# Orders of TensorE, VectorE and ScalarE written out by places of one product, and MLP2 weights converted in place, in a fused attention and two-MLP kernel

## The chip, the cores and the metric

The kernel runs on one core of a Trainium2 chip. The metric is the device time of one launch in microseconds (us); the launches of the kernel before took 960.7, 959.1 and 956.2 us, median 959.1.

The engines of a core run side by side, each through its own queue in order: TensorE (PE in the profile) multiplies matrices into PSUM, VectorE (DVE) and ScalarE (ACT) work on tiles in SBUF and PSUM, GpSimd (POOL) does a few small steps, and SyncE (SP) issues the DMAs. An instruction that waits holds up all that stand behind it in the queue of its engine.

## What is computed

```python
# q, k, v: (4 batches, 8 heads, 768 positions, 64); 8 memory keys per head
for c in range(S // 32):                       # attention in chunks of 32 queries
    k_full = [mem_k, k[l_start:r_end]]         # 8 memory keys, 16 left, 32 own, 8 right
    v_full = [mem_v, v[l_start:r_end]]
    a = softmax(q_c @ k_full.T / sqrt(64))
    out[c] = a @ v_full
x = out as (3072 tokens, 512)
x = ((x @ w_a) * (x @ w_b)) @ w_out            # MLP1: 512 -> 1536 -> 512
h = x @ w_in                                   # MLP2: 512 -> 1024
solu = h * softmax(h)
ln = (solu - mean) / sqrt(var + 1e-6) * g_ln
return ln @ w_out2                             # 1024 -> 512
```

All is float32. The weights of the MLPs reach the chip as the eight-byte words of float64 numbers and are converted there. A product in float32 is made of three matmuls: each operand is cut into a high part (a rounded copy, made on ACT) and a low part (what is left, made by a subtraction on DVE), and high x low, low x high and high x high are summed in PSUM.

## The kernel before

**Tiling.** The 3072 tokens are six blocks of 512. Attention goes by 24 groups of 128 queries, four to a block; a group has the steps load, `P`, `S` (64 small matmuls), `M` (maximum, exponent), `X` (transposes of the block's result before it), `N` (sums, and a multiplication of tile `EB` on GpSimd), `T`, `V` and `L`. Blocks 0 and 1 go straight through MLP1 in twelve steps `f`, each with 128 of the 1536 hidden columns: `ab` makes x @ w_a and x @ w_b, `gate` multiplies them, ACT casts the high part `gh`, `gate_lo` makes the low part, and `x2_step` multiplies by w_out and adds up.

**Strassen steps.** Blocks 2 to 5 go as two superblocks of two blocks, by a scheme of seven products (Strassen, in Winograd's form) in place of eight, again by twelve hidden tiles: together 24 steps, g = 0 to 23. A step g has seven `s_product`s of six 128x512 matmuls each (this takes one **place** below), in the order s_1, s_2, s_6, s_7, s_5, s_3, s_4. Between them the accumulators are snapped: ACT copies after s_1, s_6 and s_5 (lines 501, 510, 519) into three rotating buffers (`part`: G0, u2, u4, so each copy needs the buffer that an earlier step's split has finished reading), and DVE adds (506, 520, 524, 530) and multiplies (the rest of 524 to 531). The two results of a step are cut into high (ACT, 495) and low (DVE, 496) parts. From g = 2 on each step also holds four **thirds** of six matmuls, that multiply the results of step pairs before it by w_out and add to `acc` (ACT copy 550, DVE add 552).

**Operands.** For the scheme the weights of each f are first combined by sums on DVE (`s1_sums`, lines 379 and 390) and cut (`s1_split`, 396 and 397) during the second block, and travel through DRAM (`wsa`, `wsb`). The x operands need sums too (`t1_sums`, 434) and splits (`x1_op`, 444 and 445): once ahead of the first superblock, from tick 64 of the second block on, and once more between the superblocks, in step g = 11 (`last`).

**MLP2's weights.** From g = 12 on, `w2_jobs_of` gives four jobs to each step. A conversion loads 128 rows (512 KB) of raw words, takes `w_abs` (ACT, 283), `w_low` (ACT, 286), `w_range` (DVE, 296 and 297), `w_sign` (304) and `w_add` (312); w_out2's pieces are multiplied by g_ln (DVE, 623); w_in2's are also combined for the seven products by `w2_sub`. `w2_store` casts (ACT, 578), subtracts (DVE, 579) and stores the piece to DRAM (`w2s`, 22 pieces); when the places in SBUF are free, `w2_place` loads each back. w_in2 comes first, w_out2 last.

**MLP2.** Twelve pairs j of token tiles: `h_load`, `h_sums` (GpSimd), `h_split` (721, 722), then seven `product`s (`h_p1`, `h_a1`, `h_a2`, `h_b1`, `h_b2`) with running maxima (DVE, 759), `soft_exp`, `soft_stats`, `soft_scale` per tile (817 to 855), `h_norm`, the transposes `t_mm` (865), a split of them (870, 871) and `o_mm`, 24 matmuls by w_out2. At the transition, the last eight thirds run among the first products of pair 0.

**What sets the order.** TensorE's order is that of the program text throughout. VectorE's and ScalarE's is so only up to line 1059; behind it, a scheduler orders these two by its own estimate of times, with a few `issue_after` lines for the jobs. Attention steps are hung on a counter that `tick()` moves on once per place.

Of the kernel before, what the change touches and what calls it, by code (L numbers as in the profile page):

```python
# [18 lines left out]
P = 128  # L19
# [35 lines left out]
def fused_kernel(  # L55
# [23 lines left out]
    w2s = [dram.tile([P, 2, WC], F32, name=f"w2s{i}") for i in range(14 + NF2)]  # L79
# [295 lines left out]
    def s1_sums(q):  # L375
# [6 lines left out]
        )  # L382
        z = s1[q].rearrange("p (i c) -> p i c", i=4)
# [8 lines left out]
    def s1_split(q):  # L392

        l = s1.pop(q)
        h = Z[:, 4 * WC:6 * WC]
        nc.scalar.copy(h.bitcast(F32R), l)
        nc.vector.tensor_tensor(out=l.bitcast(F32R), in0=l, in1=h, op=ALU.subtract)
        for k, t in enumerate((h, l)):
            t = t.rearrange("p (i c) -> p i c", i=4)
            nc.sync.dma_start(wsa[q][:, 2:4, k], t[:, 0:4:3])  # L400
            nc.sync.dma_start(wsb[q][:, 0:2, k], t[:, 1:3])
# [24 lines left out]
    def t1_sums():  # L426

        a, b = stage(0), stage(1)
        t1, t2, t4 = (
            ld_tile(2 * TB, "t").rearrange("d (k t) -> d k t", k=2) for _ in range(3)  # L430
        )
        for o, p, q in ((t1, b[:, 0:2], a[:, 0:2]), (t2, b[:, 2:4], t1),
                        (b[:, 0:2], b[:, 2:4], b[:, 0:2]), (t4, a[:, 2:4], t2)):
            nc.vector.tensor_tensor(out=o, in0=p, in1=q, op=ALU.subtract)
        xsrc.update({2: t2, 3: t1, 5: b[:, 0:2], 6: t4})

    def x1_op(i):
# [5 lines left out]
        h, l = xop(i)[:, 0], xop(i)[:, 1]  # L443
        nc.scalar.copy(h, src)
        nc.vector.tensor_tensor(out=l, in0=src, in1=h.bitcast(F32), op=ALU.subtract)
# [14 lines left out]
    def sb_buffers():  # L460
        held["z"] = z_tile([P, NS * 2 * WC], F32R, "gz")
        held["u2"] = g_tile(1, F32, "u2")
        held["u4"] = g_tile(2, F32, "u4")
        held["h"] = g_tile(3, F32R, "g5h")
        held["l"] = g_tile(4, F32R, "g5l")
        held["acc"] = [x_tile(2 + i, F32, "acc") for i in range(2)]
# [26 lines left out]
    def s_split(g, half, src):  # L493
# [4 lines left out]
    def s_1(g, bank=None):  # L498
        cur["x"] = s_bank(bank)
        s_product(cur["x"], g, 0, 0, 0, True, False)  # L500
        nc.scalar.copy(part(g, 0), cur["x"])  # L501
# [863 lines left out]
```

## Time and profile before

| | before |
|---|---|
| launches | 960.7, 959.1, 956.2 us (median 959.1) |
| the profiled execution | 956.56 us, span 954.8 us |
| TensorE busy | 906.4 us, 95% |
| VectorE busy | 656.0 us, 69% |
| ScalarE busy | 377.3 us, 40% |
| GpSimd busy | 81.0 us, 8% |
| moved by DMA | 164.67 MB, mean 172 GB/s |

The profile is of one execution. TensorE's matmuls are pipelined: a 128x512 matmul shows about 0.39 us, but the next one starts 0.23 us after it. In the rows, a line is written `start, duration, engine, line, operation, out<-in` and, in brackets, the idle time of the engine just before it and what ended that.

### The profile page before, as it was taken

To read this page: it belongs to the slowest core of one execution; us is meant where nothing else is said; L and a number is where in the kernel's file an instruction comes from. 1 tells how busy PE (TensorE), PEld (TensorE's weight loads), DVE (VectorE), ACT (ScalarE), POOL (GpSimd) and SP (SyncE) were. 2 spreads that over 40 slices of the span, in tenths; PEclk is the share of its full clock that TensorE was granted. 3 is DMA by queue.
4 is the path that set the end of the run, shared out by engine and by line. 5 is a ranking of instruction groups with operands and counts; after the bars stand their busy time and mean duration, and the time that the engine had idled before them with its cause. 6 is when DMAs were issued, how large, how long until landed. Compare 5 with 4: busy or idle time off the path is not lost.

```text
span 954.8 us, 16795 instructions
## 1 busy us (share of the span) xinstructions
PE 906.4 (95%) x6936; PEld 740.5 (78%) x6936; DVE 656.0 (69%) x1124; ACT 377.3 (40%) x561; POOL 81.0 (8%) x97
## 2 busy tenths in 40 slices
PE   3899999999989999999899899999989999999998
PEld 3788878777767888888677677777878888888887
DVE  5999956676785445655976577877597667767661
ACT  3767633342343422222533434343243444444331
POOL 0000000000000000000000000004042222220000
PEclk9999999999999999999999999999999999999999
DMA  9993435566666445543468777876411111110001
GB/s 375 421 407 132 150 106 185 192 197 216 219 203 249 165 146 188 169 148 116 154 225 311 256 267 295 302 264 216 177 44 45 45 56 45 45 45 23 32 24 45
DMA packets 59388, 164.67 MB, mean 172 GB/s; under 512 B 4912, under 2 KB 32816, under 8 KB 54576
## 3 DMA queue, kind: packets, MB, share of 16 engines
q1 hardware_dynamic: 59280, 163.60, 48.7%
q8 instruction: 54, 0.88, 0.4%
q14 instruction: 22, 0.18, 0.1%
q0 software_dynamic: 32, 0.00, 0.0%
HBM read 117.44 MB, written 46.14 MB: 171 GB/s over the span
## 4 chain that ended last, share of the span: by engine, by line
PE 58%; issue 25%; DVE 12%; ACT 2%; DMA 1%; POOL 1%; SPq 0%; ACTq 0%; POOLq 0%; DVEq 0%
PE acc L743 11%; PE acc L481 11%; PE pab L885 5%; PE pab L883 5%; PE pab L884 5%; PE pab L644 4%; PE pab L645 4%; PE pab L646 4%; PE px L251 2%; PE pst L865 2%; DVE Z L312 2%; DVE Z L304 2%; PE s L186 2%; DMA qkv<-qkv_dram 1%; DVE G L659 1%
## 5 line engine op out<-in xcount | busy, mean ns | idle before, releaser
L481 PE MATMUL acc<-w 128*128 128x512 f32 x978 | 239.7, 393 | 13.0 <-ACT u L501 7.5
L481 PEld LDWEIGHTS acc<-w 128*128 128x128 f32 x978 | 181.4, 188 | 55.1 <-ACT u L501 9.7
L743 PE MATMUL acc<-w 128*128 128x512 f32 x360 | 87.3, 394 | 0.0
L644 PE MATMUL pab<-x,w 128*128 128x512 f32 (+1 forms) x200 | 79.9, 400 | 1.2 <-ACT x L272 0.9
L743 PEld LDWEIGHTS acc<-w 128*128 128x128 f32 x360 | 67.3, 189 | 13.9
L645 PE MATMUL pab<-x,w 128*128 128x512 f32 (+1 forms) x200 | 77.6, 388 | 0.1
L646 PE MATMUL pab<-x,w 128*128 128x512 f32 (+1 forms) x200 | 77.5, 387 | 0.0
L883 PE MATMUL pab<-w 128*128 128x512 f32 (+1 forms) x200 | 76.5, 382 | 0.0
L885 PE MATMUL pab<-w 128*128 128x512 f32 (+1 forms) x200 | 76.3, 381 | 0.0
L884 PE MATMUL pab<-w 128*128 128x512 f32 (+1 forms) x200 | 76.1, 381 | 0.0
L871 DVE TENSOR_TENSOR w<-pst,w 128x1024 fp32r<-128x1024 f32 x24 | 29.2, 1216 | 62.9 <-ACT w L870 62.9
L705 POOL TENSOR_TENSOR w2ld<-w2ld 128x256 f32<-128x256 f32 x48 | 45.3, 965 | 308.7 <-PE pab L646 203.6
L552 DVE TENSOR_TENSOR acc<-pab,acc 128x512 f32<-128x512 f32 x72 | 49.3, 688 | 14.0 <-PE pab L646 13.4
L217 POOL TENSOR_TENSOR EB<-EB,sm 128x512 f32<-128x512 f32 x18 | 19.5, 1082 | 424.5 <-DVE sm L216 424.5
L644 PEld LDWEIGHTS pab<-x,w 128*128 128x128 f32 x200 | 38.5, 192 | 9.6 <-ACT x L272 1.2
L646 PEld LDWEIGHTS pab<-x,w 128*128 128x128 f32 x200 | 38.4, 192 | 7.5
L645 PEld LDWEIGHTS pab<-x,w 128*128 128x128 f32 x200 | 38.6, 193 | 7.1 <-DVE x L277 0.4
L885 PEld LDWEIGHTS pab<-w 128*128 128x128 f32 x200 | 37.6, 188 | 7.2
L884 PEld LDWEIGHTS pab<-w 128*128 128x128 f32 x200 | 37.6, 188 | 7.1
L883 PEld LDWEIGHTS pab<-w 128*128 128x128 f32 x200 | 37.6, 188 | 7.0
L644 PE MATMUL pab<-gz,w 128*128 128x512 f32 x96 | 37.8, 394 | 1.2 <-DVE acc L552 1.2
L743 PE MATMUL acc<-w2x,w 128*128 128x512 f32 x144 | 38.8, 406 | 0.0
(193 smaller groups left out, 1718.3 us busy)
## 6 DMA issues: line engine op xcount, KB each, us to landing
w<-wsa SPq DMA_DIRECT2D x24, 1024.0 KB, 5.0
w<-wsb SPq DMA_DIRECT2D x24, 768.0 KB, 4.5
raw<-w1d_dram SPq DMA_DIRECT2D x11, 1536.0 KB, 20.5
qk<-qkv_dram SPq DMA_DIRECT2D x20, 640.0 KB, 4.6
w2s<-w2ld SPq DMA_DIRECT2D x22, 512.0 KB, 4.0
v<-qkv_dram SPq DMA_DIRECT2D x20, 512.0 KB, 3.9
w<-w2s SPq DMA_DIRECT2D x18, 512.0 KB, 6.2
wsa<-w SPq DMA_DIRECT2D x24, 256.0 KB, 2.8
```

The costliest lines, as they stand in the source:

```text
L217: (eng or nc.gpsimd).tensor_tensor(out=e, in0=e, in1=sm.to_broadcast([P, H, CK]), op=ALU.mult)
L481: nc.tensor.matmul(ps, w[:, u, k], xx[:, v, k], start=(start and k == 0 and i == 0), stop=(stop and k == 1 and i == 2), skip_group_check=True,
L552: nc.vector.tensor_tensor(out=a[:, d], in0=ps, in1=a[:, d], op=ALU.add)
L644: nc.tensor.matmul(ps, wl, xh, start=first, stop=False)
L645: nc.tensor.matmul(ps, wh, xl, start=False, stop=False)
L646: nc.tensor.matmul(ps, wh, xh, start=False, stop=last)
L705: nc.gpsimd.tensor_tensor(out=s4[:, i], in0=a, in1=b, op=op)
L743: nc.tensor.matmul(ps, x, y, start=(start and k == 0 and i == 0), stop=(stop and k == 1 and i == 2), skip_group_check=True,)
L871: nc.vector.tensor_tensor(out=ll, in0=pt, in1=lh.bitcast(F32), op=ALU.subtract)
L883: nc.tensor.matmul(po, s["lh"][:, f], wl, start=(f == 0), stop=False)
L884: nc.tensor.matmul(po, s["ll"][:, f], wh, start=False, stop=False)
L885: nc.tensor.matmul(po, s["lh"][:, f], wh, start=False, stop=(f == NF2 - 1))
```

## The change

Behind line 1059 nothing is left to the scheduler until the softmax of tiles 4 and 5 in MLP2: VectorE and ScalarE, like TensorE, follow the text. The text is written by places; `at(t, fn)` hangs any step on a place, with 72 places for the second block and eleven to a step g (`STEP`). Steps that were one function are cut so that each engine's part can have a place of its own: `s_split` into `s_hi` and `s_lo`, `third` into `third_mm` and `third_add`, `x1_op`, `s1_split`, `h_split` likewise.

Moved: the sums and splits of the x operands, from one row into places 65 to 77, and from g = 11 into g = 10, 11 and 12; the second product of the first step pair; the attention groups (regular places in the second block and steps 2 to 9); the split of h of pair 1, to between thirds; `p1(3)` behind `o_mm(0)`. The snaps of step 0 use other PSUM and SBUF buffers.

MLP2's weights: w_out2's eight pieces go first (g = 13 to 16), still by way of DRAM, with the multiplication by g_ln now on ACT. w_in2's fourteen pieces follow (g = 17 to 22) and are written straight to where MLP2 reads them (`w2_spot`), with no store and no load back: 22 stores and 22 loads become 8 and 8. Raw loads are issued in the step before (`g - 1`, places 3 and 5).

```diff
-    in_order.close()
-    in_order.enter_context(tc.manual_schedule(engines={ENG.PE}))
...
-    w2s = [dram.tile([P, 2, WC], F32, name=f"w2s{i}") for i in range(14 + NF2)]
+    w2s = [dram.tile([P, 2, WC], F32, name=f"w2s{i}") for i in range(NF2)]
...
+    def s_hi(g, half):
+        nc.scalar.copy(gbuf(g % NF1, half)[0], part(g, (1, 2)[half]))
+
+    def s_lo(g, half):
         h, l = gbuf(g % NF1, half)
-        nc.scalar.copy(h, src)
-        nc.vector.tensor_tensor(out=l, in0=src, in1=h.bitcast(F32), op=ALU.subtract)
+        nc.vector.tensor_tensor(
+            out=l, in0=part(g, (1, 2)[half]), in1=h.bitcast(F32), op=ALU.subtract
+        )
...
+    def w2_hi(name, n):
+        if name >= 14:
+            nc.scalar.activation(
+                out=w2_z(n), in_=w2_z(n), func=AF.Copy, scale=gln_sb[:, name - 14:name - 13]
+            )
+            w2_dst[name] = w2_spot(name % 4)
+        else:
+            w2_dst[name] = w2_spot(next_of("spot", 14))
+        nc.scalar.copy(w2_dst[name][:, 0], w2_z(n))
...
+    for t, fn, i in (
+        (65, t1_sum, 0), (66, t1_sum, 1), (67, x1_hi, 2), (68, x1_lo, 2), (69, t1_sum, 2),
...
+    STEP = 11
+
+    def sb_time(g, k):
+        return 72 + STEP * g + k
...
+    for n, k in enumerate((0, 2, 3, 4)):
+        at(sb_time(10, k), t1_sum, n)
+    for i, h, l in (
+        (0, 1, 2), (1, 2, 4), (2, 3, 6), (5, 5, 8), (3, 7, 11), (4, 9, 14), (6, 11, 16)
+    ):
+        at(sb_time(11, h), x1_hi, i)
+        at(sb_time(11, l), x1_lo, i)
...
+    def sb_conversions(g, ops):
+        times = ((-1, -1, 0, 1, 2, 2, 3), (1, 2, 3, 4, 4, 5, 6))
+        for b, (src, n, name) in enumerate(ops):
+            t = [sb_time(g, k) for k in times[b]]
+            at(sb_time(g - 1, (3, 5)[b]), w2_load, src, b)
+            at(t[0], lambda b=b, n=n: w_abs(w2_raw(b), w2_z(n)))
+            at(t[1], lambda b=b: w_low(w2_raw(b)))
...
+        s_product(x, g, 0, 0, 0, True, False)
+        if g:
+            s_lo(g - 1, 0)
+        nc.scalar.copy(part(g, 0), x)
+        tick()
...
+        s_product(v, g, 1, 2, 6, False, True)
+        ring_load(g + 2, 1)
+        s_vec(g, 1, v, part(g, 1), ALU.add)
+        s_vec(g, 1, part(g, 0), part(g, 1), ALU.mult)
+        tick()
+        if g > 1:
+            third_mm(u + 3)
+            third_add(u + 3)
+        s_hi(g, 0)
+        tick()
...
+    units(5)
+    h_split(1, (1,))
+    h_a2v(0)
...
+    h_b2(0)
+    soft_exp(1)
+    h_a1w(1)
+    soft_mult(0)
+    h_a1w_max(1)
...
+    o_mm(0)
+    t_mm(1)
+    soft_stats(3)
+    h_p1(3)
```

Three places of the two programs, in the order in which an engine meets its instructions. First ScalarE in a step that converts a piece of w_in2, before: 283 and 286 are the conversion, 495 the cast of a result of the step, 501 and 510 the snaps of the first and third product of the next step (`acc` into the rotating buffers u and G).

```order
L495 CAST w<-u_3019 128x512
L550 COPY acc<-pab 128x512
L495 CAST w<-u_3018 128x512
L283 ACTIVATE w2ld<-w2ld 128x512
L286 ACTIVATE w2ld<-w2ld 128x512
L501 COPY u_3019<-acc 128x512
L510 COPY G_124<-acc 128x512
```

The same after: 518 is the cast of a result, 1241, 1250 and 1260 are the three snaps, 283 and 286 as before, 603 the cast into the place in SBUF that MLP2 reads.

```order
L518 CAST g5h<-G_110 128x512
L518 CAST gz<-u_2975 128x512
L283 ACTIVATE AT<-w2ld 128x512
L286 ACTIVATE w2ld<-w2ld 128x512
L1241 COPY G_110<-acc 128x512
L283 ACTIVATE w2ld<-w2ld 128x512
L1250 COPY u_2974<-acc 128x512
L603 CAST w2x<-AT 128x512
L286 ACTIVATE w2ld<-w2ld 128x512
L1260 COPY u_2975<-acc 128x512
```

The first conversion of a step still stands ahead of the snap of the first product (501, now 1241); the second one is spread between the snaps.

Second, ScalarE where the x operands are renewed for the second superblock, before: 444 casts an operand, 495 a result, 519 and 501 are snaps.

```order
L444 CAST w<-t 128x1024
L519 COPY G_124<-acc 128x512
L444 CAST w<-xs 128x1024
L283 ACTIVATE EB<-w2ld 128x512
L286 ACTIVATE w2ld<-w2ld 128x512
L283 ACTIVATE EB<-w2ld 128x512
L286 ACTIVATE w2ld<-w2ld 128x512
L444 CAST w<-t 128x1024
L495 CAST g5h<-G_124 128x512
L495 CAST gz<-u_3019 128x512
L501 COPY G_124<-acc 128x512
```

The same after, with 463 the cast of an operand:

```order
L1241 COPY u_2974<-acc 128x512
L463 CAST w<-xs 128x1024
L1250 COPY u_2975<-acc 128x512
L463 CAST w<-xs 128x1024
L463 CAST w<-t 128x1024
L1260 COPY G_110<-acc 128x512
L463 CAST w<-xs 128x1024
L518 CAST g5h<-G_110 128x512
L463 CAST w<-t 128x1024
L463 CAST w<-xs 128x1024
L518 CAST gz<-u_2975 128x512
L1241 COPY G_110<-acc 128x512
```

The casts of operands stand between the snaps, at most two in a row, and no conversion stands among them.

Third, VectorE at the transition, around the softmax of the first token tile, before: 828 multiplies by the exponentials, 831 are statistics, 839, 840 and 846 make the scale `v` with a step of GpSimd between 840 and 846, 759 are maxima of the next pair, 855 applies the scale, and the transposes of tile 0 on TensorE wait for it.

```order
L839 TENSOR_SCALAR v<-mv,r 128x1
L840 TENSOR_SCALAR v<-v 128x1
L828 TENSOR_TENSOR acc<-acc,he 128x1024
L835 TENSOR_SCALAR r<-ssum 128x1
L846 TENSOR_TENSOR v<-v,r 128x1
L759 ISA acc,mx<-acc,zero_63,mx 128x512
L759 ISA mx 128x1
L831 BN_STATS stats<-acc 128x6 x2
L855 TENSOR_SCALAR acc<-acc,mv,v 128x1024
L836 RECIPROCAL r<-r 128x1
```

The same after, where 860, 877, 883, 893 are the steps that were 828, 840, 846, 855, 729 a split of pair 2's h and 768 the maxima:

```order
L876 TENSOR_SCALAR v<-mv,r 128x1
L877 TENSOR_SCALAR v<-v 128x1
L860 TENSOR_TENSOR acc<-acc,he 128x1024
L729 TENSOR_TENSOR w<-w2ld,w 128x1024
L768 ISA acc,mx<-acc,u_2975 128x512
L768 ISA mx 128x1
L883 TENSOR_TENSOR v<-v,r 128x1
L893 TENSOR_SCALAR acc<-acc,mv,v 128x1024
```

The statistics of the next tile (831) no longer stand ahead of the scaling of tile 0, and a split of pair 2 does; the transposes of tile 0 themselves have moved behind the products p1(2), b1(1) and b2(1) on TensorE.

## Rows read from the trace of the kernel before

**Rows 1.** Windows: stretch, us; PE, PEld, DVE, ACT, POOL busy; clock; DMA share, GB/s.
```profile
151.50:290.00 138.50, 131.65 (x1539) 105.31 (x1540) 101.57 (x157) 49.91 (x74) 8.43 (x8) 0.99 0.61 199
290.00:464.00 174.00, 173.32 (x1722) 140.24 (x1721) 93.48 (x149) 55.15 (x94) 8.96 (x8) 1.00 0.48 161
464.00:495.00 31.00, 26.01 (x113) 20.55 (x112) 24.11 (x38) 10.88 (x18) 0.00 (x0) 1.00 0.59 198
495.00:657.00 162.00, 152.00 (x660) 122.80 (x659) 117.72 (x196) 62.74 (x110) 4.39 (x5) 1.00 0.77 271
...
698.00:712.00 14.00, 10.99 (x46) 8.76 (x45) 13.49 (x35) 6.67 (x11) 5.45 (x6) 0.88 0.14 45
712.00:954.80 242.80, 239.55 (x1172) 200.91 (x1170) 153.66 (x358) 93.20 (x139) 39.79 (x50) 1.00 0.11 40
```

**Rows 2.** Waits of TensorE by what ended them: total, times, longest.
```profile
PE acc L481 <- ACT u L501: 7.5, 4, 2.4
...
PE pst L865 <- DVE r L836: 3.0, 1, 3.0
```

**Rows 3.** Windows around the two stretches of lower clock.
```profile
148.00:151.00 3.00, 1.79 (x69) 1.41 (x67) 1.00 (x3) 1.76 (x5) 0.00 (x0) 1.00 0.75 235
151.00:154.50 3.50, 3.42 (x73) 2.87 (x73) 1.19 (x3) 0.00 (x0) 0.00 (x0) 0.53 0.60 192
...
704.00:707.40 3.40, 3.40 (x11) 2.72 (x10) 3.32 (x10) 2.67 (x4) 2.98 (x4) 0.52 0.19 51
```

**Rows 4.** Timeline of ScalarE at a w_in2 conversion (540 to 547).
```profile
542.83 0.66 ACT L283 ACTIVATE w2ld<-w2ld 128x512 f32<-128x512 f32 x1 [2.15 <-DMA w2ld<-win_dram]
543.39 0.64 ACT L286 ACTIVATE w2ld<-w2ld 128x512 int32<-128x512 uint32 x1
543.93 0.57 ACT L501 COPY u<-acc 128x512 f32<-128x512 f32 x1
```

**Rows 5.** Timeline of TensorE at the same place.
```profile
539.75 2.43 PE L481 MATMUL acc<-w 128*128 128x512 f32 x10
544.55 1.65 PE L481 MATMUL acc<-w 128*128 128x512 f32 x6 [2.38 <-ACT u L501]
```

**Rows 6.** The page's groups of instructions: busy, mean ns, idle time before.
```profile
L481 PE MATMUL acc<-w 128*128 128x512 f32 x978 | 239.7, 393 | 13.0 <-ACT u L501 7.5
```

**Rows 7.** Timeline of ScalarE at the renewal of operands (471 to 478).
```profile
472.00 1.05 ACT L444 CAST w<-t 128x1024 fp32r<-128x1024 f32 x1
...
475.00 0.62 ACT L495 CAST gz<-u 128x512 fp32r<-128x512 f32 x1 [1.43 <-DVE u L531]
476.20 0.58 ACT L501 COPY G<-acc 128x512 f32<-128x512 f32 x1 [0.58 <-DVE g5l L496]
```

**Rows 8.** Timeline of VectorE late in the second block (266 to 275).
```profile
272.79 1.22 DVE L445 TENSOR_TENSOR w<-t,w 128x1024 fp32r<-128x1024 f32 x1
273.93 0.68 DVE L659 TENSOR_TENSOR G<-G,pab 128x512 f32<-128x512 f32 x1
```

**Rows 9.** Timeline of VectorE at the transition (696 to 704).
```profile
701.07 1.28 DVE L831 BATCH_NORM_STATS2 stats<-acc 128x6 f32<-128x512 f32 x2
702.26 0.80 DVE L855 TENSOR_SCALAR acc<-acc,mv,v 128x1024 f32<-128x1024 f32 x1
```

**Rows 10.** One line's instructions: min/median/max ns, first and last start, form.
```profile
L217 POOL TENSOR_TENSOR EB<-EB,sm x18: 1043/1046/1375, 119.5 to 445.5; 128x512 f32<-128x512 f32 x18
L623 DVE TENSOR_SCALAR EB<-EB,gln_sb x4: 476/478/489, 583.4 to 624.5; 128x512 f32<-128x512 f32 x4
```

**Rows 11.** Groups of ScalarE's instructions by line: busy, mean ns, idle before.
```profile
L495 ACT CAST gz<-u 128x512 fp32r<-128x512 f32 x16 | 9.9, 620 | 30.5 <-DVE u L524 18.2 <-DVE u L531 12.3
```

**Rows 12.** Landing times of the sixteen raw loads of MLP2's weights (line 565).
```profile
DMA to landing us min/median/max: 3.7/5.1/8.1
```

**Rows 13.** Windows of 22 us around the transition.
```profile
690.30:712.00 21.70, 18.69 (x80) 15.13 (x79) 21.00 (x50) 11.62 (x20) 9.37 (x10) 0.92 0.15 48
712.00:734.00 22.00, 22.00 (x107) 18.37 (x106) 18.01 (x45) 9.21 (x15) 5.69 (x7) 1.00 0.14 49
```

More of the change, by code (lines that the diff above doesn't have):

```diff
@@ L1118, in fused_kernel @@
             ring_load((f - 9) // 2, 1)
-    while events:
-        tick()
-    units = iter(range(48 * NSB))
-    done_units = 0
-    def unit(n=1):
-        for _ in range(n):
-            third(next(units))
-            tick()
-    def later(job):
-        def run():
-            with tc.issue_after(cur["last"].ins):
-                job()
-        return run
-    jobs = w2_jobs_of()
-    clock = 0
+    assert clock == 72
+    STEP = 11
+    def sb_time(g, k):
+        return 72 + STEP * g + k
@@ L1139, in fused_kernel @@
         sb, f = divmod(g, NF1)
-        if g == 0:
-            att_load(q0 + 8)
-            attention(q0 + 8, 26, 12.2)
-        last = sb + 1 < NSB and f == NF1 - 1
-        if last:
-            while events:
-                tick()
-            t1_sums()
-        def renew(i):
-            if last:
-                x1_op(i)
-        if sb == NSB - 1:
-            if f == 0:
-                held["ld"] = [ld_tile(2 * WC, "w2ld") for _ in range(3)]
-            for n in range(4):
-                if jobs:
-                    events.setdefault(clock + 1 + 3 * n, []).append(later(jobs.pop(0)))
@@ L1210, in wo2_place @@
-    def wo2_place():
-        spots = [AB(i)[:, 1024 * n:1024 * n + 1024] for i in (9, 10, 2, 3) for n in range(2)]
-        for f, r in enumerate(spots):
-            w2_place(14 + f, r)
     def prepare(j):
@@ new lines, in fused_kernel, with units @@
+    w2_place(20, WO(8).rearrange("p h c -> p (h c)"))
+    w2_place(21, WO(9).rearrange("p h c -> p (h c)"))
+    u = 4 * (NSB * NF1 - 2)
+    def units(n, add=None):
+        third_mm(u + n)
+        if add is not None:
+            third_add(u + add)
+    units(0)
+    units(1, 0)
+    h_p1(0)
+    third_add(u + 1)
+    units(2)
+    h_split(1, (0,))
+    units(3, 2)
+    h_a1w(0)
+    third_add(u + 3)
+    h_a1w_max(0)
+    units(4)
+    h_split(1, (2,))
+    h_a1x(0)
+    third_add(u + 4)
+    units(5)
@@ L1265, in fused_kernel @@
+    h_a2x(1)
+    h_a2max(1)
     soft_scale(0)
     h_norm(0)
-    h_b2(0)
-    soft_exp(1)
-    with tc.issue_after(st2[0]["last"].ins):
-        soft_stats(1)
-    soft_scale(1)
-    ha(1)
-    hb(1)
-    t_mm(0)
-    ha(2)
+    h_p1(2)
+    h_b1(1)
+    h_b2(1)
+    soft_exp(2)
+    soft_stats(1)
+    t_mm(0)
+    h_a1w(2)
+    h_a1w_max(2)
+    h_a1x(2)
+    soft_scale(1)
+    h_norm(1)
+    h_split(2, (2,))
+    soft_mult(2)
+    h_sums(3)
+    h_a2v(2)
+    h_a2x(2)
+    soft_exp(3)
+    h_a2max(2)
@@ new lines, in fused_kernel @@
+    h_split(3, (0,))
+    soft_stats(2)
+    soft_scale(2)
+    soft_mult(3)
+    h_split(3, (1,))
+    o_mm(0)
+    t_mm(1)
+    soft_stats(3)
+    h_p1(3)
+    soft_scale(3)
+    h_split(3, (2,))
+    h_load(4)
+    h_b(2)
+    for t in (4, 5):
+        last = soft_exp(t)
+    in_order.close()
+    in_order.enter_context(tc.manual_schedule(engines={ENG.PE}))
+    in_order.enter_context(tc.issue_after(last[0].ins))
+    in_order.enter_context(tc.issue_after(last[1].ins))
+    for t in (4, 5):
+        soft_mult(t)
+        soft_stats(t)
+        soft_scale(t)
```

513 lines of the change are left out of this document (280 added, 233 removed).

## Prediction

> **What bounds the kernel now.** The page comes first: TensorE is busy 95% of the span, so a change can win by filling its waits, or by taking matmuls away, and this one takes none away. The windows tell where the waits are, width less TensorE's busy time [rows 1]: 6.85 us in the second block and the first steps (151.5 to 290), 0.68 until 464, 4.99 where the x operands are renewed (464 to 495), 10.00 in the steps that convert MLP2's weights (495 to 657), none until 698, 3.01 at the transition (698 to 712), 3.25 behind it. What is behind 712 keeps its order nearly, and what is ahead of 151.5 is the same code. So **25.5 us** are in reach. The list of waits then says who ends them: the largest entries that lie behind 151.5 are a ScalarE copy (line 501) and one wait of 3.0 for VectorE [rows 2]. Last, two stretches have the clock at half its level: windows of 3.5 and 3.4 us at 0.53 and 0.52 [rows 3], which cost 3.5 x 0.47 = 1.65 and 3.4 x 0.48 = 1.63 us beyond any idle time.
>
> The timelines show the mechanism, the same each time: a queue in order, with work that nobody waits for at its head. At 542.83 ScalarE sits 2.15 us waiting for raw weights, then runs 283 and 286, and only then the copy 501 [rows 4], for which TensorE has waited 2.38 us [rows 5]. At the renewal, casts of 1.05 us and results that wait for VectorE stand ahead of copy 501 [rows 7]. In the second block, VectorE runs a row of 1.22-us operand sums and splits, and the addition 659 that TensorE wants comes behind them [rows 8]. At the transition the statistics of the next tile run ahead of the scaling 855 of the first [rows 9].
>
> One price is used throughout. Ten matmuls in a row show 2.43 us [rows 5] and one of them 0.393 [rows 6], so each starts (2.43 - 0.39)/9 = 0.227 us after the one ahead of it; a place of six is 1.36 us, a step of eleven places 14.96.
>
> **Second block and first steps (6.85 us).** The operands' sums and splits now stand one or two to a place, which takes away the waits of the kind in rows 8. What stays, by the new order: (a) the first T comes six places behind its S, and GpSimd's multiplication of 1.05 us [rows 10] is then the last of its inputs: 0.65 us. (b) At three places the cast of `gh` stands ahead of the attention copy that V needs; a cast is 0.62 [rows 11], about 0.30 of it hidden: 3 x 0.32 = 0.96. (c) Steps 0 and 1 have no thirds between their products. From step 0's last product to the copy in step 1 stand, in a chain, three VectorE operations of 0.68 [rows 8], a cast of 0.62 [rows 11], a copy of 0.58 [rows 7] and four hand-overs of 0.05 (the copy ends at 544.50, TensorE starts at 544.55 [rows 4, 5]): 3.44 us, against two products, 2.72: 0.72 late. (d) From step 1 to 2 an attention copy of 0.58 is added: 1.3. Together 3.63, **gain 3.2**; bounds 0 (the same waits at other places) and 6.85.
>
> **Up to 464 (0.68 us).** Attention groups have a place or more to spare at each step: **gain 0.7**; it can't be more, and a lost place would cost about as much.
>
> **Renewal (4.99 us).** The four sums move to g = 10 and the seven casts are spread over g = 11 and 12, at most two between two snaps: 2 x 1.05 [rows 7] fits beside two places, 2.72. VectorE has seven splits of 1.22 [rows 8], 8.5 us, over two steps of 14.96, beside some 8.8 of its own in each. The first conversion is a step away, so no raw weights are waited for. **Gain 5.0**, from 3.5 if a cast still lands ahead of a snap in one place.
>
> **Weight conversions (10.00 us).** There are eight steps with two conversions each. A raw load is issued at place 3 or 5 of the step before and used seven places on, 9.5 us later, less some 0.7 for the issue and what stands ahead: 8.8. Landings of the same loads took 3.7 to 8.1 us [rows 12], so the 2.15 us of rows 4 go. The snap of the first product still stands behind a cast, 283 and 286. Counted from the start of the eleventh place: add and multiply 1.36, cast 0.62, the two conversions 0.55 each (start to start in rows 4), copy 0.58, hand-overs 0.25: 3.9 us, against three places, 4.08. So there is 0.14 to 0.2 us to spare, no more; at the two steps where ScalarE also has copies of thirds I get 0.27 too little. A margin so thin will not hold everywhere: I charge 0.2 at six steps and 0.27 at two, 1.75. By the same durations I count 13.4 us of work for VectorE in the fullest such step of 14.96; it just keeps up. **Gain 8.2**; bounds 2 (VectorE falls behind by 1 us at each of the eight steps) and 10.
>
> Less DMA traffic (14 pieces neither stored nor loaded, 14 MB of 164.67) is worth nothing on TensorE by itself: no wait of TensorE in these steps is for `w2s`. The moved multiplication by g_ln takes eight times 0.48 us from VectorE [rows 10] and gives ScalarE eight operations; the nearest rows on that engine are 0.62 [rows 11] and 0.66 [rows 4]. It lies beside TensorE's work. The Trainium skill's ScalarE: Activation LUTs (What ACT_TABLE_LOAD costs) adds 93 ns for an operand of one value per partition, an estimate of 0.71 us, and the sum would be the same.
>
> **Transition (3.01 us and 1.63 of clock).** VectorE is the tight engine here: 21.00 of 21.70 us, then 18.01 of 22.00 [rows 13]. Without TensorE's wait the same 39.0 us of work would stand in 40.7. So 1.7 us of slack serve all hand-overs to TensorE, and reordering can't make more of it, only choose who is late. By the new order I see four hand-overs that come late: o_mm(1) 1.1, t_mm(2) 0.7, a product of pair 3 1.0, o_mm(2) 1.3, together 4.1; since one wait also gives the next its time, 3.2. All are shorter than the 2.38 us behind which no low clock followed, so I take the second low stretch as gone. **Gain 3.01 + 1.63 - 3.2 = 1.4**; bounds -2 (waits of 5, clock still low) and 4.6. The first low stretch (151 us) follows code that doesn't change, and stays.
>
> The rows and the rule on the clock: ahead of the first low stretch TensorE was busy 1.79 of 3.00 us, ahead of the second it stood for 3.0 [rows 3, 2], and 2.38 us at 542 left the clock alone. The Trainium skill's TensorE: Matmul & The Clock Gate (HAM oscillation) has idle gaps of the engine lower the clock; by that alone, shorter waits give back the 1.63 us and several short ones close together might not. With it kept low the sum would be 1.6 us worse.
>
> **Sum.** 3.2 + 0.7 + 5.0 + 8.2 + 1.4 = 18.5 us. From the profiled execution, 956.6 - 18.5 = 938.1; from the median, 959.1 - 18.5 = 940.6. The profiled one is 2.5 us below the median but beside the fastest launch; I take **939.0**, nearer to it.
>
> **Rivals.** *Clean*: nearly all waits go, at the transition too, and only some 1 us is left. 956.6 - 25.5 - 1.6 + 1 = 930.5. For it speaks that my margins count every duration in full, where neighbours on an engine overlap by some 0.1 us (283 shows 0.66 and the next starts 0.56 after it [rows 4]); against it, VectorE's 39.0 of 40.7 us. *VectorE becomes the bound* in the steps of conversion and at the transition: everything on it is now in order, so one late operation delays all behind. At 1 us for each of eight steps (in place of 1.75 in all, so 6.25 more) and 2 more at the transition: 939.0 + 8.3 = 947. For it speak 13.4 of 14.96 us; against it, that before it took the same work without being what ended the long waits [rows 2 to 5]. *Slower: ScalarE waits for raw weights.* 283 stands ahead of a snap at each of sixteen loads, and nothing can pass it now. A snap may be late by a place less its copy, 1.36 - 0.58 = 0.78 us. To lose the 20.1 us between 939.0 and the median and 4.8 more, each load must cost 24.9/16 = 1.56, so land 8.8 + 0.78 + 1.56 = 11.1 us after its issue, all sixteen; there the time is 964, and beyond it slower. Against it: the worst of sixteen was 8.1 [rows 12], and DMA has less to do than before. *It doesn't do what it says*: waits go from one place to another, and the time stays at 958.
>
> **How the numbers follow.** A measurement of this kernel tells about 0.5%, 4.8 us, from no change. Forecast 0.49 (with its margins, 933 to 944), clean 0.20, VectorE 0.20, unchanged 0.06, slower 0.05. So faster 0.89, same 0.06, slower 0.05. The range is to hold the forecast, most of clean and of VectorE: 929.5 to 950.
>
> **What would show it.** TensorE's waits: none over 1 us between the second block's end and 657; no wait for 283's successors; the renewal free of waits; at the transition several waits of about 1 us ended by VectorE's split of the transposes, and the clock full. If the forecast is wrong by the VectorE rival, the waits in conversion steps are ended by VectorE's adds (lines 506 to 531 as they are now), growing through a step; if by the ScalarE rival, ScalarE's own list of waits shows the raw loads, as 2.15 in rows 4. If the transition's waits are gone altogether, my count of hand-overs was too dark, and the time is near 931 to 936.

## Result and the profile after

The changed kernel takes **931.4 us** (median of four launches, 931.1 to 931.6), against 957.65 (956.1 to 960.7): a ratio of 0.972, 95% interval 0.969 to 0.975. The forecast was 939.0, range 929.5 to 950; the time is near that of the rival called *clean* (930.5). The span fell from 954.8 to 929.7 us, by 25.1. One launch of all that follow, of the variant with pieces in the raw buffers, took 4462 us and is left out.

The windows of the profile after, by the same stages as [rows 1]; columns as there:

```profile
151.50:290.00 138.50, 134.49 (x1587) 107.82 (x1588) 104.06 (x158) 51.54 (x78) 13.15 (x8) 1.00 0.64 212
290.00:460.00 170.00, 168.91 (x1693) 136.87 (x1671) 94.28 (x147) 52.32 (x89) 8.36 (x8) 1.00 0.47 156
460.00:490.00 30.00, 30.00 (x134) 24.77 (x133) 23.56 (x34) 12.28 (x19) 0.00 (x0) 1.00 0.60 205
490.00:648.00 158.00, 157.83 (x694) 129.32 (x693) 123.36 (x201) 70.05 (x119) 5.94 (x8) 1.00 0.61 209
...
690.00:705.00 15.00, 14.98 (x74) 12.25 (x72) 13.51 (x32) 7.99 (x14) 3.96 (x6) 1.00 0.19 67
705.00:929.70 224.70, 220.25 (x1076) 184.20 (x1074) 141.91 (x328) 85.08 (x127) 38.32 (x48) 1.00 0.11 41
```

Width less busy time of TensorE: 4.01 and 1.09 us are left of the second block and the first steps (6.85 before), none of the renewal (4.99), 0.17 of the conversions (10.00), 0.02 and 1.18 of the transition (3.01; the other 3.27 of the last window's 4.45 are the tail, 3.25 before). The clock column is full in every row. What still stops TensorE, by its waits over the whole span (four of the eight for line 229, 2.3 us, lie behind 151.5):

```profile
PE px L251 <- ACT AT L229: 5.7, 8, 1.2
...
PE acc L505 <- ACT u L1241: 1.6, 2, 1.1
PE pt L227 <- POOL EB L217: 1.2, 2, 0.8
...
PE pab L922 <- DVE w L909: 0.7, 1, 0.7
...
PE acc L752 <- ACT u L764: 0.5, 1, 0.5
```

Line 501 with its 7.5 us and line 865 with 3.0 [rows 2] have no counterpart of that size: the snap is now line 1241, 1.6 in all, at steps 1 and 2, and the transposes wait for nothing. At a w_in2 conversion, where ScalarE sat 2.15 us and TensorE 2.38 [rows 4, 5], ScalarE and then TensorE now read:

```profile
541.68 0.62 ACT L518 CAST gz<-G 128x512 fp32r<-128x512 f32 x1 [2.40 <-DVE G L527]
542.21 0.67 ACT L283 ACTIVATE EB<-w2ld 128x512 f32<-128x512 f32 x1
542.78 0.67 ACT L286 ACTIVATE w2ld<-w2ld 128x512 int32<-128x512 uint32 x1
543.36 0.56 ACT L1241 COPY u<-acc 128x512 f32<-128x512 f32 x1
```

```profile
541.39 4.94 PE L505 MATMUL acc<-w 128*128 128x512 f32 x21
```

The row on ScalarE is the same, cast, 283, 286, snap; the raw words are there, and TensorE runs 21 matmuls without a break across it.

**The account of 25.1 us.** Idle time behind 151.5 us fell from 25.5 to 6.5: 19.0. A stop costs more than its idle time: a matmul shows 0.393 us [rows 6], and the next could have started at 0.227, so 0.166 of every stop is counted as busy (the drained pipeline, below). The stops behind 151.5 went from 21 to 12: 1.5 us. Both low stretches of the clock [rows 3] are missing: 3.3. Ahead of 151.5, where the code is the same, the last wait for line 229 starts 0.6 us sooner (147.84 in place of 148.44). That is 24.4; 0.7 is not assigned.

### The profile page after: what moved, and what is told of

Same layout as the page of the kernel before. It is cut to its first block, busy times and chain, and to the rows that moved or that the text cites. A ratio compares the mean times of both kernels' runs of the same rounds, so it can differ in the third digit from the quotient of the medians.

```text
span 929.7 us, 16746 instructions
## 1 busy us (share of the span) xinstructions
PE 900.5 (97%) x6936; PEld 738.1 (79%) x6936; DVE 657.8 (71%) x1116; ACT 382.0 (41%) x569; POOL 81.5 (9%) x97
## 2 busy tenths in 40 slices
DMA packets 55356, 149.98 MB, mean 161 GB/s; under 512 B 4464, under 2 KB 32368, under 8 KB 50544
## 4 chain that ended last, share of the span: by engine, by line
PE 75%; DVE 12%; DMA 6%; issue 4%; ACT 2%; POOL 0%; SPq 0%; DVEq 0%; ACTq 0%; POOLq 0%
PE acc L505 23%; PE acc L752 10%; PE pab L646 7%; PE pab L647 7%; PE pab L648 7%; DMA raw<-w1d_dram 4%; PE pab L922 4%; PE pab L923 4%; PE pab L921 4%; PE px L251 2%; PE pst L903 2%; DVE Z L304 1%; DVE Z L312 1%; PE s L186 1%; DMA qkv<-qkv_dram 1%
## 5 line engine op out<-in xcount | busy, mean ns | idle before, releaser
L527 DVE TENSOR_TENSOR u<-acc,u 128x512 f32<-128x512 f32 x61 | 42.0, 689 | 44.9 <-PE acc L505 30.3
L707 POOL TENSOR_TENSOR w2ld<-w2ld 128x256 f32<-128x256 f32 x48 | 41.5, 885 | 301.1 <-DVE w2ld L312 183.5
L217 POOL TENSOR_TENSOR EB<-EB,sm 128x512 f32<-128x512 f32 x18 | 23.6, 1311 | 400.6 <-DVE sm L216 400.6
L752 PE MATMUL acc<-w2x,w 128*128 128x512 f32 x144 | 42.5, 403 | 0.5 <-ACT u L764 0.5
```

Source lines behind the costliest of these rows:

```text
L527: nc.vector.tensor_tensor(out=part(g, o), in0=a, in1=b, op=op)
L707: nc.gpsimd.tensor_tensor(out=s4[:, i], in0=a, in1=b, op=op)
L752: nc.tensor.matmul(ps, x, y, start=(start and k == 0 and i == 0), stop=(stop and k == 1 and i == 2), skip_group_check=True,)
```

## Experiments

Ratios are to the kernel before in the same series, whose median lay between 957.6 and 958.8. All variants are made from the changed kernel.

**The changed kernel again.**

> The changed kernel once more, as the base that its variants are compared with. Expected 931.4 us within 0.4, with 8.4 us lost at stops of TensorE behind 151.5 us of the span (idle time and the drained pipeline, start to start). On the clock: if the stretch at half clock that stood at 151 us before is tied to the code behind it, this profile shows none there, as the first profile of the changed kernel; if it comes by chance, it may be there again, and the time is 1.6 us longer.

932.0 us (930.9 to 933.1), ratio 0.972 (0.970 to 0.975), span 929.4. Every stop behind 151.5 came back at the same place and within 0.03 us of its size. There is again no low clock at 151. That is chance: of the thirteen profiles with this code up to there (the first of the changed kernel, and the twelve runs of this section), five do have it. Of the four launches here, two have a mean clock of 1.000 and took 930.9 and 931.2, two have 0.998 and took 932.7 and 933.1. The window from 151 to 154.5 of the run with raw loads later in the text (below), and of the changed kernel:

```profile
151.00:154.50 3.50, 3.50 (x79) 3.11 (x78) 1.40 (x3) 0.25 (x1) 0.00 (x0) 0.63 0.59 181
```

```profile
151.00:154.50 3.50, 3.50 (x88) 3.27 (x87) 2.14 (x3) 1.15 (x2) 0.00 (x0) 1.00 0.79 246
```

So some 1.6 us of the 25.1 are luck of the profiled execution, not the change.

**The pieces written over the raw words again.**

```diff
+        if b is not None:
+            spot[name] = w2_dst[name]
+            w2_dst[name] = held["ld"][b].bitcast(F32R).rearrange("p (h c) -> p h c", h=2)
         nc.scalar.copy(w2_dst[name][:, 0], w2_z(n))
...
-        if name >= 14:
-            nc.sync.dma_start(w2s[name - 14], w.bitcast(F32))
+        if name >= 14 or name in spot:
+            nc.sync.dma_start(w2s[name], w.bitcast(F32))
+        if name < 14 and name in spot:
+            at(clock + 8, w2_back, name)
...
-            at(sb_time(g - 1, (3, 5)[b]), w2_load, src, b)
+            at(sb_time(g - 1, ((3, 7), (5, 7))[g == 20][b]), w2_load, src, b)
...
```

> The changed kernel, but eighteen of the 22 pieces of MLP2's weights (all but the last four of w_in2) are written over the raw words as before, stored to DRAM and, those of w_in2, loaded back to their places eight places later; the orders of ScalarE and VectorE are the same. A raw load can then be issued only when the store of the piece that sits in its buffer has landed. Theory (conversion in place gained by freeing the raw buffers sooner; in the kernel before, raw loads waited for stores 18.3 us in all, ten times): the load of a step's first conversion goes out about place 7, 4.8 us ahead of its use, that of the second about place 10, 2.7 us ahead; with landings of 3.6 to 8.6 us ScalarE waits for raw loads with the snap behind it, 1 to 2 us at each of eight steps: 939 to 948. Rival (the order alone gained it): within 1.5 us of 931.5, with no raw load among ScalarE's waits.

955.2 us (953.3 to 957.6), ratio 0.997 (0.995 to 0.999): **nearly the whole gain is gone** with this one part undone, more than the theory had said. (The traffic that comes back with it, and the later places of the loads in the text, cost nothing by themselves, as the next two runs show.) ScalarE, TensorE and the DMA queue (SPq) at one of the steps:

```profile
502.78 0.66 ACT L283 ACTIVATE AT<-w2ld 128x512 f32<-128x512 f32 x1 [2.90 <-DMA w2ld<-wout_dram]
503.34 0.66 ACT L286 ACTIVATE w2ld<-w2ld 128x512 int32<-128x512 uint32 x1
503.90 0.56 ACT L1253 COPY u<-acc 128x512 f32<-128x512 f32 x1
```

```profile
504.52 3.89 PE L505 MATMUL acc<-w 128*128 128x512 f32 x10 [2.72 <-ACT u L1253]
```

```profile
491.35 4.82 SPq L617 DMA_DIRECT2D w2s<-w2ld  x2
499.07 0.33 SPq L593 DMA_DIRECT2D w2ld<-wout_dram  x1
...
500.29 0.33 SPq L593 DMA_DIRECT2D w2ld<-wout_dram  x1
```

The raw load goes out at 499.07 only, 3.7 us ahead of its use at 502.78, since the stores of the pieces that sat in the raw buffers came first. The queue's own list of waits says the same of the kernel before and of the changed one:

```profile
SPq L565 <- DMA w2s<-w2ld: 18.3, 10, 4.9
```

```profile
SPq L593 <- DVE EB L312: 26.9, 8, 5.9
```

Before, a raw load waited for a store to land; now it mostly waits for the operation that reads the raw words last (312). Six stops of 17.0 us idle stood in the conversion steps of the variant, with low clock at two of them. One of the six is 7.2 us, behind a raw load issued at 604.48 only, after the pieces of a step of sums; and 6.8 us of low clock from 150.5 on, in this profile, stand ahead of all that the variant changes. In the kernel before, a 283 that had waited for raw words stands ahead of four of the stops in these steps, 6.3 of the 10.0 us; one more, of 1.5 us, stands behind a cast of h (721) that waited for GpSimd. That late loads cost less there because the scheduler placed work around them by its estimate is my reading; no run shows it.

**The traffic back, the buffers free.**

```diff
+    w2e = [dram.tile([P, 2, WC], F32, name=f"w2e{i}") for i in range(14)]
...
+        else:
+            nc.sync.dma_start(w2e[name], w.bitcast(F32))
+            if clock + 8 < 72 + 11 * 24:
+                at(clock + 8, nc.sync.dma_start, w.bitcast(F32), w2e[name])
```

> The changed kernel, but each of the fourteen pieces of w_in2 is stored to DRAM as it is written and, for all but those finished last, loaded back onto its own place eight places later: the traffic that the change took away, with the orders of the engines as they are. Theory (the order gained it, the traffic is worth nothing): 931.4 within 1 us, and landing times of the raw loads up by less than 2 us. Rival (converting in place and the lighter DMA queues brought a part of the 11 us gained in the conversion steps): stops come back in the steps g = 17 to 22, and the time is 934 or more.

931.3 us (931.2 to 932.3), ratio 0.972 (0.969 to 0.974): no change, the stops are those of the changed kernel. The traffic (149.98 MB moved, 163.62 here) is worth nothing; what the variant before this one lost came from the buffers that were not free.

**Raw loads later in the text.**

```diff
-            at(sb_time(g - 1, (3, 5)[b]), w2_load, src, b)
+            at(sb_time(g - 1, (7, 9)[b]), w2_load, src, b)
```

> The changed kernel, but the raw loads of MLP2's weights are issued at places 7 and 9 of the step before, not 3 and 5: 5.4 us later. In the changed kernel the first load of a step was issued 10.8 to 11.5 us before its use, the second 8.2 to 8.7, and they landed in 3.6 to 8.6 us (median 4.8). Theory (the slower rival's mechanism is real, ScalarE waits with the snap behind it): the second loads are late by about 4.8 - 3.0 = 1.8 us, less 0.78 that a snap may be late, eight times 1.0, and some of the first loads: 936 to 945, with ScalarE's own list of waits showing the raw loads. Rival (landings are hidden anyway, and TensorE's waits in the kernel before came from the order alone): 931 to 933.

931.8 us, ratio 0.971 (0.967 to 0.976), but it tells nothing on the question: the loads were issued at the same times as in the changed kernel (485.7 became 486.7, in a trace that lies 1.0 us later there). Here the DMA queue is not ordered by the text, and the load went when its buffer was free. It does say that the places 3 and 5 in the text set nothing.

**Raw loads held back.**

```diff
-            at(sb_time(g - 1, (3, 5)[b]), w2_load, src, b)
+            at(sb_time(g - 1, (7, 9)[b]), lambda b=b: nc.vector.memset(held["ld"][b][:, 0:1], 0.0))
+            at(sb_time(g - 1, (7, 9)[b]), w2_load, src, b)
```

> The changed kernel, but a small write by VectorE into the raw buffer stands at places 7 and 9 of the step before, and holds the raw load back to there: moving the load's place in the text alone had left its issue where it was, since its queue is not ordered by the text. Theory (the slower rival's mechanism is real: ScalarE waits for raw words with the snap behind it): the second load of a step now has about 3.0 us, the first 5.4; with landings of 3.5 to 8.6 us (median 4.5) that is 0.7 to 1 us of stop at each of the eight steps for the second and some for the first: 936 to 945. Rival (a snap may be late enough that landings are hidden anyway): 931 to 933.

952.4 us, ratio 0.994 (0.991 to 0.997): 21 us lost, past the upper end of what was expected (1.6 of it, in the profile, is the low clock at 151). ScalarE at one step; two of its operations wait for raw words, and a snap stands behind each (1242, 1251):

```profile
503.20 0.66 ACT L283 ACTIVATE AT<-w2ld 128x512 f32<-128x512 f32 x1 [0.71 <-DMA w2ld<-wout_dram]
...
507.93 0.66 ACT L283 ACTIVATE w2ld<-w2ld 128x512 f32<-128x512 f32 x1 [3.04 <-DMA w2ld<-wout_dram]
508.50 0.57 ACT L1251 COPY u<-acc 128x512 f32<-128x512 f32 x1
```

TensorE's idle time in these steps came to 14.2 us over nine stops, 0.166 more for each, and 3 us of low clock. The size was missed because both loads of a step were late, and because of the clock: in the window behind a stop of 2.38 us it reads 0.55.

```profile
555.00:559.50 4.50, 2.12 (x10) 1.44 (x9) 1.95 (x4) 1.69 (x3) 0.00 (x0) 1.00 0.84 318
559.50:563.00 3.50, 3.50 (x11) 2.68 (x10) 2.35 (x6) 2.27 (x4) 0.00 (x0) 0.55 0.03 7
```

**The margin at the snap.**

```diff
-            at(t[0], lambda b=b, n=n: w_abs(w2_raw(b), w2_z(n)))
+            for _ in range(3 - 2 * b):
+                at(t[0], lambda b=b, n=n: w_abs(w2_raw(b), w2_z(n)))
```

> The changed kernel, but the first operation (283) of the first conversion in each of the eight conversion steps is run three times on ScalarE, with the same result: 1.1 us more work ahead of the snap of the next step's first product. Theory (the prediction's margin is right: 0.17 us to spare at six of these steps, none at two): each stops TensorE for the rest, 6 x 0.93 + 2 x 1.1 = 7.8 us, so 939. Rival (the margin is larger than worked out, ScalarE has time enough): 1 to 4 us.

942.6 us (942.1 to 943.3), ratio 0.983 (0.979 to 0.987): 11 us, more than 7.8. ScalarE and TensorE at the step shown above:

```profile
498.37 2.06 ACT L283 ACTIVATE AT<-w2ld 128x512 f32<-128x512 f32 x3
```

```profile
501.51 1.89 PE L505 MATMUL acc<-w 128*128 128x512 f32 x7 [1.14 <-ACT u L1242]
```

Three take 2.06 us, so two more are 1.38, not 1.1. Six steps stop for 1.06 to 1.14 us idle, 1.23 to 1.30 with the 0.166: the margin is 1.38 less that, 0.08 to 0.15 us, where 0.17 was worked out. The two steps with copies of thirds stop for 1.47, 1.63 with it: 0.25 too little, where 0.27 was worked out. All eight stops end at the snap, as the theory says.

**Scheduler's order from the first step on.** VectorE and ScalarE left to the scheduler behind place 72, MLP2's weights tied as before.

```diff
+        if t >= 72 + 11 * 13 - 1:
+            run = lambda: after_last(lambda: fn(*a))
...
     assert clock == 72
+    in_order.close()
+    in_order.enter_context(tc.manual_schedule(engines={ENG.PE}))
...
```

> The changed kernel, but VectorE and ScalarE are ordered by the scheduler again from the first step (g = 0) to the end; the work on MLP2's weights is again tied behind the last addition or product of a step, as in the kernel before. TensorE's order, the places in the text, the early loads and the pieces in place stay. The transition alone in the scheduler's hands gave 939.2. Theory (the order of these two engines by hand is what gained in the steps): the stops of the renewal and of the conversions come back besides, at least half of the 16.9 us of before, so 947 to 957. Rival (places, early loads and conversion in place gained it): within 2 us of 939.2.

942.4 us (941.5 to 944.7), ratio 0.983 (0.979 to 0.987).

**Scheduler's order at the transition only.**

```diff
     s_lo(NSB * NF1 - 1, 0)
+    in_order.close()
+    in_order.enter_context(tc.manual_schedule(engines={ENG.PE}))
     w2_place(20, WO(8).rearrange("p h c -> p (h c)"))
...
```

> The changed kernel, but VectorE and ScalarE are ordered by the scheduler again from the end of the last step on, that is at the transition and behind it; TensorE's order and the places in the text stay. Theory (at the transition the order written by hand for these two engines is what gained): stops of 2 to 4 us in all come back there, perhaps with a stretch of half clock (1.6): 934 to 937. Rival (the gain there is from TensorE's order and from splits of pairs 1 and 2 standing earlier in the text): within 1 us of 931.4.

939.2 us (938.6 to 940.2), ratio 0.980 (0.977 to 0.982). The two belong together. They are 3.2 us apart, with intervals of their ratios that overlap, and 3.0 in their spans, of which 1.6 is the low clock at 151 that only the first one's profile has. In the steps, TensorE stops seven times for 3.6 us in the first, and twice for 1.6 in the second. So in 24 steps the order by hand is worth 1 to 3 us, where at least half of 16.9 was expected: **my theory for the steps falls**. What is left, by elimination, is the places, the freed buffers and the text cut into parts, which gain with the scheduler as well; the buffers were tested above, the places only at the renewal, below, and the cutting of the text by no run. At the transition the order by hand is worth 7.8 against the scheduler's order of the same text, more than the 2.5 to 5.5 that I had said. That includes some 1.8 us of low clock behind the long wait (0.58 of the full one from 685.66 to 690.00). TensorE's transposes of tile 0, and VectorE ahead of them, in the second variant:

```profile
685.66 1.73 PE L903 MATMUL pst<-ident,acc 128*128 128x128 f32 x7 [5.47 <-DVE acc L893]
```

```profile
683.98 0.68 DVE L883 TENSOR_TENSOR v<-v,r 128x1 f32<-128x1 f32 x1 [0.70 <-POOL v L878]
684.70 0.81 DVE L893 TENSOR_SCALAR acc<-acc,mv,v 128x1024 f32<-128x1024 f32 x1
```

The scaling 893 comes at 684.70 there; by the hand-written order it ends 0.15 us ahead of the transposes, which do not stop:

```profile
676.39 1.19 DVE L893 TENSOR_SCALAR acc<-acc,mv,v 128x1024 f32<-128x1024 f32 x1
```

```profile
677.73 1.06 PE L903 MATMUL pst<-ident,acc 128*128 128x128 f32 x8
```

What TensorE's own new order gives at the transition (the transposes behind three products more) was not run by itself.

**The renewal in a row.**

```diff
-    for n, k in enumerate((0, 2, 3, 4)):
+    for n, k in enumerate((10, 10, 10, 10)):
         at(sb_time(10, k), t1_sum, n)
     for i, h, l in (
-        (0, 1, 2), (1, 2, 4), (2, 3, 6), (5, 5, 8), (3, 7, 11), (4, 9, 14), (6, 11, 16)
+        (0, 1, 1), (1, 2, 2), (2, 3, 3), (5, 5, 5), (3, 7, 7), (4, 9, 9), (6, 11, 11)
```

> The changed kernel, but the x operands are renewed as before: the four sums in one row at the end of step 10, and each low part at the place of its high part. Theory (a row of work that nobody waits for at the head of VectorE's queue is what stopped TensorE at the renewal): the row is 4 x 1.14 = 4.6 us ahead of additions and products that the next step needs within 2.7, so stops of 2 to 4 us in steps 10 to 12, 933.5 to 936. Rival (the renewal stopped in the kernel before because conversions stood in the same step, and these are a step away now): within 1 us of 931.5.

934.7 us (two launches), ratio 0.974 (0.968 to 0.980), with the low clock at 151 in its profile. Two stops came back, 0.37 us and the one below, 2.5 us in all with the 0.166 each; expected were 2 to 4.

```profile
472.32 1.89 PE L505 MATMUL acc<-w 128*128 128x512 f32 x7 [1.82 <-ACT G L1241]
```

So the row of sums and splits accounts for 2.2 of the 4.99 us of idle time of before. The rest did not come back; that it came from the conversions, which stood in the same step, fits but is not shown.

**A split moved back at the transition.**

```diff
     h_a2x(0)
-    h_split(2, (0,))
...
+    h_split(2, (0,))
     soft_scale(0)
     h_norm(0)
     h_p1(2)
```

> The changed kernel, but the first part of the split of pair 2, which stands among the last thirds, is moved to just ahead of the scaling of tile 0 (VectorE 1.2 us for it). Theory (what the new text gains at the transition is that splits of later pairs are pulled ahead, into thirds where VectorE had time): in the changed kernel tile 0's transposes start 0.15 us after the scaling ends, without a stop, so they are now late by about 1 us, and the stops behind (0.5 and 0.7) change little: 932.3 to 933. Rival (VectorE has time at the transition as well): 931.5.

934.6 us (two launches), ratio 0.976 (0.973 to 0.980), 2.6 to 3.2 more than the changed kernel's two medians. The stop is not where I had put it: not the transposes wait, but the products of pair 2, for the cast (725) and the low part (729) of this split.

```profile
675.42 0.51 PE L752 MATMUL acc<-w2x,w 128*128 128x512 f32 x1 [1.25 <-ACT w L725]
677.34 0.73 PE L752 MATMUL acc<-w2x,w 128*128 128x512 f32 x2 [1.41 <-DVE w L729]
```

What is pulled ahead matters, as the theory says, through the split's own reader.

**Three small moves for a faster kernel.** The gate behind the attention steps, the casts of steps 0 and 1 behind the next snap, 286 behind the snap:

```diff
+        tick()
         gh, gl = gate(f, pab[1])
-        tick()
...
-        times = ((-1, -1, 0, 1, 2, 2, 3), (1, 2, 3, 4, 4, 5, 6))
+        times = ((-1, 0, 0, 1, 2, 2, 3), (1, 2, 3, 4, 4, 5, 6))
...
-        if g:
+        if g > 2:
             s_lo(g - 1, 0)
         nc.scalar.copy(part(g, 0), x)
+        if 0 < g <= 2:
+            s_hi(g - 1, 0)
+            s_lo(g - 1, 0)
...
-        s_hi(g, 0)
+        if g > 1:
+            s_hi(g, 0)
```

> The changed kernel with three small moves: in the second block the gate's multiplication and cast are issued behind the attention steps of the same place, so that the cast no longer stands ahead of the copy that V needs; the cast of the first result of steps 0 and 1 is issued behind the first snap of the next step; the second part of the first conversion (286) behind that snap too. Theory (work at the head of a queue in order is what TensorE waits for): the stops of 0.16, 0.41 and 0.53 us (attention), 0.55 and 1.09 (steps 1 and 2), and the two of 0.08 go, with 0.16 us of drained pipeline each: 2.82 + 7 x 0.16 = 3.9 us, so 927.5. Rival (the engine is short of time there, and the order only decides who is late): stops of the same sum at other places, 930.5 to 932.

929.4 us (928.4 to 929.7), ratio 0.970 (0.967 to 0.972). The seven stops that were aimed at are gone, but the gate's multiplication came late at one place (1.14 us), so 927.5 was missed. With the gate moved only where a copy for V stood behind its cast:

```diff
-        gh, gl = gate(f, pab[1])
+        if f not in (2, 6, 10):
+            gh, gl = gate(f, pab[1])
         tick()
+        if f in (2, 6, 10):
+            gh, gl = gate(f, pab[1])
```

> The variant with three small moves again, but the gate's multiplication and cast go behind the attention steps only where a copy for V stood behind the cast (f = 2, 6, 10). There the moves took away the five stops they were aimed at and the two of 0.08, but where the gate goes behind the attention steps everywhere, VectorE's multiplication came late once (1.14 us) and the wait for GpSimd grew from 0.76 to 1.09. Theory: those two go back, the others stay away: 0.8 us less, so a span of 925.8, 0.4% under the changed kernel. Rival: new collisions of the same size, 926.6 or more.

**927.3 us** (927.1 to 927.6), ratio 0.969 (0.966 to 0.971), span 925.3; expected 925.8. That is below every launch of the changed kernel (930.9 to 933.1 in all) and of the variant before this one. Its windows of the second block and of the conversions:

```profile
151.50:290.00 138.50, 136.14 (x1603) 109.52 (x1593) 105.46 (x160) 52.19 (x78) 13.17 (x8) 1.00 0.65 215
...
490.00:648.00 158.00, 158.00 (x698) 130.50 (x697) 121.91 (x198) 70.33 (x120) 5.95 (x8) 1.00 0.63 216
```

## Why the prediction was right, and where it was not

**What bounds it: right.** TensorE's waits behind 151.5 were most of it: 19.0 of the 25.5 us in reach went. The sum said 18.5 in all and was 6.6 short. By the account above, 2.1 of that are waits (19.0 against 16.9, which is 18.5 less the 1.63 of clock), 1.5 the drained pipeline, 1.65 the clock at 151, 0.6 the earlier start, and 0.7 stays open. That the time came out at *clean* is luck in part: that rival left 1 us of waits and 6.5 stayed, and terms that it did not have, some of them chance, made up for most of it.

**Second block and first steps: too optimistic, by 1.5 us.** Left are 5.10 (4.01 and 1.09), not 3.63. Term (b), three places where a cast stands ahead of V's copy, 0.96: measured 0.16, 0.41 and 0.53, 1.10. Terms (c) and (d), 0.72 and 1.3: measured 0.55 and 1.09. The causes of (b), (c) and (d) are shown, since moving these casts took the stops away. Term (a) was mis-sized: 0.65 was charged for GpSimd at one T, and there are two such stops, 0.40 and 0.76, and 1.21 for the copy behind the first. GpSimd's multiplication, taken at 1.05 [rows 10], took 1.04 at the first of them and 1.85 at the second (below).

**Up to 464 and renewal: right.** 0.7 and 5.0 forecast, both all gone.

**Conversions: mechanism right, 1.6 us too pessimistic.** The snap behind a cast, 283 and 286 is the tight place, with the margin as worked out (0.08 to 0.15 against 0.17, -0.25 against -0.27). What failed is the next step, the charge of 0.2 at six steps because "a margin so thin will not hold everywhere". In the two profiles of the changed kernel the stops repeat within 0.03 us; a margin of 0.08 to 0.15 that is positive cost nothing here. Also, why the loads come in time was told wrongly: not their places in the text, but the freed buffers. That part I had counted as worth nothing ("less DMA traffic ... is worth nothing on TensorE by itself"), which is true of the traffic, and I did not see that the same edit frees the buffers on which the 8.8 us rested. In the trace the second load of a step goes out 8.2 to 8.7 us ahead of its use in six of the eight steps, the first 10.8 or more in all.

**Transition: 1.4 forecast, 3.4 came.** The step that failed is "reordering can't make more of it". 39.0 us of VectorE's work in 40.7 were read from windows that begin at 690.3; in the 21.5 us ahead of them VectorE had time. That window of before, and the three of after that begin at the same third as it (VectorE is the third busy column):

```profile
668.80:690.30 21.50, 21.50 (x97) 17.80 (x96) 9.85 (x19) 4.48 (x7) 0.00 (x0) 1.00 0.51 188
```

```profile
646.30:667.80 21.50, 21.50 (x96) 17.64 (x95) 12.43 (x22) 5.26 (x9) 2.87 (x4) 1.00 0.55 196
667.80:689.50 21.70, 21.70 (x101) 17.87 (x100) 19.54 (x47) 11.52 (x18) 5.34 (x6) 1.00 0.08 25
689.50:711.50 22.00, 20.79 (x98) 16.51 (x97) 20.43 (x49) 10.20 (x17) 7.00 (x10) 1.00 0.20 71
```

9.85 became 12.43, so 2.6 us of work (splits of pairs 1 and 2) are done sooner, among the thirds; the 21.7 us behind it, 21.00 before [rows 13], fell to 19.54, and the 22 us behind those rose from 18.01 to 20.43. The order within counts as well: the variant with the scheduler's order has the same text and stops for 5.47. Of the four late hand-overs (3.2 us), two stayed, 0.49 at a product and 0.69 at `o_mm(2)`. The prediction had named this case: with a count of hand-overs that was too pessimistic, the time would be near 931 to 936. That the second low clock goes with the long wait fits: it is absent here, and back where the wait is (scheduler's order at the transition).

**The clock at 151: "stays" was wrong as a statement on one profile.** It comes in some executions and not in others.

**Drained pipeline: left out.** 0.166 us for each stop, 1.5 in all. It could have been read from [rows 5, 6], which already held what it takes.

**Rivals.** *VectorE the bound* is refuted for this order: no wait in the conversion steps ends at it. *ScalarE waits for raw weights* has the price that was feared: held back, the loads cost 21 us; with pieces in the raw buffers again, 24. The changed kernel stays clear: its longest wait for raw words is 0.6 us, and no stop of TensorE stands behind it. Of the part that was to be worth nothing, the multiplication by g_ln took 0.72 us on ScalarE, where 0.71 was estimated.

## What to carry to other kernels

Before an order is written out by hand, see what frees the buffer that each early load needs: a fixed order with late loads was no faster here than the scheduler's (955.2), with early loads it was 2.8% faster. Count a stop of TensorE with the drained pipeline. A margin of 0.1 us that was positive held in this fixed order, so look at the trace before charging for one. Where one stage is tight for an engine, look at the stage ahead of it for room before calling the stage full.

## What the hardware showed beside it

**GpSimd and VectorE hold each other up.** GpSimd's 217 multiplies two tiles in SBUF. In the changed kernel it took 1.82 to 1.85 us six times out of eighteen, and 1.05 else; each of the six begins 0.2 us or so behind VectorE's 411, a subtraction with both inputs in SBUF. GpSimd, VectorE and the T on TensorE that waits:

```profile
240.84 1.85 POOL L217 TENSOR_TENSOR EB<-EB,sm 128x512 f32<-128x512 f32 x1 [14.47 <-DVE sm L216]
...
254.26 1.85 POOL L217 TENSOR_TENSOR EB<-EB,sm 128x512 f32<-128x512 f32 x1 [11.56 <-DVE sm L216]
```

```profile
240.62 1.17 DVE L411 TENSOR_TENSOR Z<-Z 128x1024 fp32r<-128x1024 f32 x1
...
255.12 2.07 DVE L379 TENSOR_TENSOR Z<-w 128x1024 f32<-128x1024 f32 x1
```

```profile
242.75 0.66 PE L227 MATMUL pt<-ident,EB 128*128 128x128 f32 x4 [0.76 <-POOL EB L217]
```

411 ends at 241.79, and 217 needs another 0.90 from there. The other way round, 379, whose inputs are in SBUF too, takes 2.07 us in place of 1.22 where it begins inside a 217 (254.26 to 256.10). The Trainium skill's SBUF — State Buffer (Who interferes with whom) says that a VectorE instruction with two SBUF inputs contends with a GpSimd instruction that reads SBUF, and that the order of issue decides who blocks. These rows agree.

**The clock after stops of the same length.** A stop of 2.38 us left the clock alone in the kernel before [rows 5], and one of 2.38 us was followed by a low stretch with the raw loads held back; all profiles have stops of 0.73 and 0.47 us between 147 and 150.5 (some one more, of up to 0.38), and a low stretch followed in the kernel before and in five of thirteen profiles of its successors, with that one and without. The length of a stop alone did not tell here.
